# Packed attention with a top-1 mixture of experts: one count of tokens per expert behind the last batch, and the branch behind the loop with its sides exchanged

## The chip, the cores and the metric

The kernel runs on one core of a Trainium2 chip. The metric is the device time of one execution in microseconds (us); lower is better. Engines are named as the profile names them: PE is TensorE (PEld its weight loads), DVE is VectorE, ACT is ScalarE, POOL is GpSimd, SP is SyncE, which here only issues DMAs and waits. A name with a q (SPq, ACTq) is the engine's sequencer: waits, branches, register loads and DMA issues, which don't count as busy.

## The reference, cut to what matters

```python
def sm_attn(qq, kk, vv):
    s = scale * np.matmul(qq, kk.transpose(0, 1, 3, 2))
    a = np.exp(s - np.max(s, axis=-1, keepdims=True))
    a = a / (np.sum(a, axis=-1, keepdims=True) + 1e-09)
    return np.matmul(a, vv)
p_packed = sm_attn(p, k, v)          # batch 8, heads 8, 32 packed rows, head size 64
x = sm_attn(q, p_packed, p_packed)   # 576 tokens a batch, then (4608, 512)

expert_idx = np.argmax(xn @ en.T / tau, axis=1)   # 8 experts; xn, en: rows divided by their norms
for e in range(E):
    mask = expert_idx == e
    h = np.maximum(x[mask] @ w1[e], 0.0)
    out[mask] = gate_w[mask, None] * (h @ w2[e])
```

With these inputs the expert that the kernel guesses for a batch is that of all its 576 tokens: in the trace nothing of the path for missed tokens runs.

## The kernel before

The kernel takes the 8 batches one after the other. For each it **guesses** the expert of the whole batch from the packed rows (`guess`), runs that expert's feed-forward for all 576 tokens on PE (`ffn`), and lays the next batch's attention between the matmuls (`att1`, `att2`). `att2` ends with `route`, which computes for every token the logits of 8 experts and the sum of squares, and from them a one-hot matrix `oh` of the token's true expert. `gates` makes the gate weights of it.

Whether the guess held is checked. Per batch, `counts` multiplies a column of ones with `oh` in two small matmuls (L732: 32 columns, L735: 8 columns), so that PE adds up the tokens per expert into a PSUM tile of the ring `pf` (4 buffers), and DVE adds the five pieces (L737). `gates_main` then multiplies with the one-hot row `sel` of the guess (L1231) and sums (L1232) into `rest_f[b]`. Behind the loop DVE turns these into tokens that the guess missed (L1372 to L1378), and all five engines load the total into a register (L1379) and branch on it (L1380): over 0, a second, slow path runs batch by batch; at 0, which is the case here, the program ends. The slow path ("rest path" below) is a few hundred instructions an engine that stand in the program though none of them runs.

The order of the work is set by Python generators that are stepped by hand. `ffn` yields after every few matmuls and the loop at L1324 to L1369 steps the next batch's attention there; for batch 0 a table `PLAN` says which generator is stepped. All instructions are put out in that order and each engine runs its own in order. The names that the change and the prediction touch:

- `route` (L657 to L725): ten times a batch DVE reduces logits out of a PSUM tile `pt` (L695), and ACT squares the other columns of the same tile with a sum (L699; the trace shows it as an ACTIVATE and an ACTIVATION_READ_ACCUMULATOR). The squares themselves go to a tile `scr` that nothing reads; it has 2 buffers. ACT's square waits for DVE's reduce of the same piece, and DVE's next reduce out of the same PSUM bank waits for ACT's square.
- `w1_rows` (L831 to L857): PE multiplies packed rows with the first weights (L841), ACT takes the high part `G` (L854) and DVE the rest (L855), in turn, four times.
- `key_scores` (matmuls on L259 with `kt`): the first scores of a batch's attention; its second half writes the PSUM tile that the last L855 reads.
- `keys` (L284 to L286 on DVE): transposes of a batch's keys, which free the buffers `nat` into which SP loads (L174, L200). SP issues all its DMAs in order.
- At the end each engine that takes the branch at L1380 clears its semaphores (SP nine of them, each waiting for that queue's last DMA) and goes to the end block (L1479), where SP waits once more for everything and a barrier of all engines closes the program.

Of the kernel before, what the change touches and what calls it, by code (L numbers as in the profile page):

```python
# [17 lines left out]
P = 128  # L18
HB = 4
NC5 = 5  # L20
# [3 lines left out]
def kernel(  # L24
# [55 lines left out]
    for e in range(E):  # L80
        nc.vector.memset(ecol[:, e : e + 1], float(e))
    rest_f = cp.tile([1, B], F32, name="rest_f")
    rest_i = cp.tile([1, B + 1], I32, name="rest_i")

    def rsqrt(x, y, tag, eng=nc.vector):
# [66 lines left out]
    class Batch:  # L152
        def __init__(self):
            for name in ("kT", "qT", "s1", "mx", "p1", "sums", "rinv", "pp2", "s2", "p1T"):
                setattr(self, name, {})
            self.begun = self.soft = False

    def load_nat(b, n):

# [362 lines left out]
    def guess(x, late=0, engine=mybir.EngineType.Pool, total=None):  # L522
        pt = ps.tile([P, 512], F32, name="pu", tag="pf")
        if total is not None:

            for n in range(NPR):
                nc.tensor.matmul(
                    pt[:1, :E], total[:, n : n + 1], enT[:, n], start=(n == 0), stop=(n == NPR - 1)
                )
        else:  # L530
            for g in range(NG):
                nc.tensor.matmul(pt[:1, :E], itau, x.ppf[:, g, D:], start=(g == 0), stop=(g == NG - 1))
        yield
        m8 = sm.tile([1, 8], F32, name="m8", tag="m8")
        idx = sm.tile([1, 8], U32, name="idx", tag="idx")
        nc.vector.max(m8, pt[:1, :E])
        nc.vector.max_index(idx, m8, pt[:1, :E])
        gi = sm.tile([1, 1], F32, name="gi", tag="gi")
        nc.vector.tensor_copy(gi, idx[:, 0:1])
        x.sel = sm.tile([1, E], F32, name="sel", tag="sel")  # L540
        nc.vector.tensor_scalar(
            out=x.sel, in0=ecol[:1], scalar1=gi, scalar2=None, op0=ALU.is_equal
        )
        yield from idle(late)
        x.e = nc.values_load(idx[0:1, 0:1], engines=[engine], min_val=0, max_val=E - 1)
# [126 lines left out]
    def route(x, fine=False):  # L672
        lgs, sss = x.routed
        for c0, c1 in ((0, 2), (2, NC5)):
            pts = [pb.tile([P, 1024], F32, name="pt", tag="pb") for _ in range(2)]
            for c in range(c0, c1):
                for g in range(NG):
                    for n in range(2 * c, min(2 * c + 2, S // 64)):
                        for h in range(HB):
                            at = 512 * (h % 2) + 256 * g + XW * (c - c0)  # L680
                            nc.tensor.matmul(  # L681
                                pts[h // 2][64 * (n % 2) : 64 * (n % 2) + 64, at : at + XW],
                                x.at[32 * h : 32 * h + 32, g, 64 * n : 64 * n + 64],
                                x.ppf[32 * h : 32 * h + 32, g],
                                start=True,
                                stop=True,
                                tile_position=(32 * h, 64 * (n % 2)),
                            )
            yield
            views = [pt.rearrange("p (b s) -> p b s", s=256) for pt in pts]  # L690
            for c in range(c0, c1):
                r = rows(c)
                for m in range(2):
                    v = views[m][:r, :, XW * (c - c0) : XW * (c - c0) + XW]
                    nc.vector.tensor_reduce(  # L695
                        lgs[:r, m, c], v[:, :, D:].rearrange("p b e -> p e b"), axis=AX.X, op=ALU.add
                    )
                    scr = sb.tile([P, 4, D], F32, name="scr", tag="scr", bufs=2)
                    nc.scalar.activation(  # L699
                        scr[:r], v[:, :, :D], AF.Square, accum_out=sss[:r, m, c : c + 1]  # L700
                    )
                yield

        lg = sm.tile([P, NC5, E], F32, name="lgt", tag="lgt")
        ss = sm.tile([P, NC5], F32, name="sst", tag="sst")
        nc.vector.tensor_tensor(out=lg, in0=lgs[:, 0], in1=lgs[:, 1], op=ALU.add)
        nc.gpsimd.tensor_tensor(out=ss, in0=sss[:, 0], in1=sss[:, 1], op=ALU.add)
        x.lg, x.ss = lg, ss
        if fine:
            yield  # L710
        nc.vector.tensor_scalar_mul(lg, lg, itau)
        mx = sm.tile([P, NC5, 1], F32, name="lmx", tag="lmx")
        nc.vector.tensor_reduce(mx, lg, axis=AX.X, op=ALU.max)
        nc.vector.tensor_tensor(
            out=lg, in0=lg, in1=mx.broadcast_to([P, NC5, E]), op=ALU.subtract
        )
        oh = sm.tile([P, NC5, E], F32, name="oh", tag="oh")
        nc.vector.scalar_tensor_tensor(
            out=oh, in0=lg, scalar=0.0, in1=code.broadcast_to([P, NC5, E]),
            op0=ALU.is_ge, op1=ALU.mult,  # L720
        )
        nc.vector.tensor_reduce(mx, oh, axis=AX.X, op=ALU.max)
        nc.vector.tensor_tensor(
            out=oh, in0=code.broadcast_to([P, NC5, E]), in1=mx.broadcast_to([P, NC5, E]),
            op=ALU.is_equal,  # L725
        )
        x.oh = oh

    def counts(x):
        oh = x.oh  # L730
        pt = ps.tile([P, 512], F32, name="pu", tag="pf")
        nc.tensor.matmul(  # L732
            pt[:1, : 4 * E], ones, oh[:, 0:4].rearrange("p c e -> p (c e)"), start=True, stop=True
        )
        nc.tensor.matmul(pt[:1, 4 * E : 5 * E], ones[:64], oh[:64, 4], start=True, stop=True)  # L735
        cnt = sm.tile([1, E], F32, name="cnt", tag="cnt")
        nc.vector.tensor_reduce(  # L737
            cnt, pt[:1, : 5 * E].rearrange("p (c e) -> p e c", c=NC5), axis=AX.X, op=ALU.add
        )
        x.cnt = cnt  # L740


    def gates(x, eng=nc.vector):
# [263 lines left out]


    bat = [Batch() for _ in range(B)]
    NAT = 2 * NPR + NG  # L1010
    seq = [(b, i) for b in range(1, B) for i in range(NAT)]
    seq[NPR : 2 * NPR + NG] = [(1, i) for i in (8, 9, 4, 5, 6, 7)]
# [20 lines left out]
    def att_main(b):  # L1033
        x = bat[b]
        if b == 1:
            prefetch(5)
            yield from keys(x, nat_main(1), pns[1])
        if b:
            if b > 1:
                counts(bat[b - 1])  # L1040
            yield from att1(x, nat_main(b), b == 1)
            if b == 1:
                expert = guess(x)
                next(expert)
                query_scores(x)
                yield
            if b > 1:
                expert = guess(x)
                next(expert)
        second = att2(x, keys_main(b + 1) if b else None, b == 0, b == 1)  # L1050
        if b == 1:
            drain(expert)
            load_w1(x, x.e, queue=nc.gpsimd)
            yield
            yield next(second)
            yield next(second)
            load_w2(x, x.e, nc.gpsimd)
            route_tiles(x)
            yield next(second)
            yield next(second)  # L1060
        elif b:
            yield next(second)
            yield next(second)
            drain(expert)
            load_w1(x, x.e, queue=nc.gpsimd)
            yield next(second)
            load_w2(x, x.e, nc.gpsimd)
            route_tiles(x)
        yield from second
        x.soft = True  # L1070
        if b == B - 1:
            yield from idle(2)
            counts(x)

    def begin():

# [150 lines left out]
    def gates_main(b):  # L1227
        x = bat[b]
        yield from gates(x, nc.vector if b else nc.gpsimd)
        hit = sm.tile([1, E], F32, name="hit", tag="hit")  # L1230
        nc.vector.tensor_tensor(out=hit, in0=x.cnt, in1=x.sel, op=ALU.mult)  # L1231
        nc.vector.tensor_reduce(rest_f[:, b : b + 1], hit, axis=AX.X, op=ALU.add)  # L1232

    def store_main(b):
        x = bat[b]
# [70 lines left out]
    def route_first():  # L1306
        route_tiles(bat[0])
        yield from route(bat[0], True)
        yield
        counts(bat[0])  # L1310

    with tc.manual_schedule():
        begun = begin()
# [55 lines left out]
                    next(gate, None)  # L1369


    nc.vector.tensor_scalar(  # L1372
        out=rest_f, in0=rest_f, scalar1=-1.0, scalar2=float(S), op0=ALU.mult, op1=ALU.add
    )
    nc.vector.tensor_copy(rest_i[:, 0:B], rest_f)
    tot = sm.tile([1, 1], F32, name="tot")
    nc.vector.tensor_reduce(tot, rest_f, axis=AX.X, op=ALU.add)
    nc.vector.tensor_copy(rest_i[:, B : B + 1], tot)  # L1378
    n_rest = nc.values_load(rest_i[0:1, B : B + 1], min_val=0, max_val=B * S)  # L1379
    with tc.If(n_rest > 0):  # L1380
        with tc.For_i(0, B, 1) as b:
            nb = nc.values_load(rest_i[0:1, ds(b, 1)], min_val=0, max_val=S)
            with tc.If(nb > 0):
# [99 lines left out]
```

## Time and profile before

| | us |
|---|---|
| median of three runs | 439.41 (438.62 to 439.89) |
| the profiled execution, device time | 438.68 |
| its span, first to last instruction | 437.1 |
| outside the span | 1.6 |
| PE busy | 417.7 (96% of the span), 4802 instructions |
| PEld busy | 351.7 (80%) |
| DVE busy | 312.6 (72%) |
| ACT busy | 217.9 (50%) |
| POOL busy | 137.5 (31%) |
| DMA | 88.36 MB, mean 202 GB/s |

Busy times are shares of the whole span and overlap. The chain of work that ended last is followed back from the last instruction that did work; waits, branches and semaphores behind it stand in the span and not in the chain. A line number is that of the kernel before.

### The profile page before, as it was taken

The numbers are of one execution on the slowest core, as the hardware profiler recorded it, in microseconds if no ns is written. First come the engines' busy times: TensorE is split into PE (matmuls) and PEld (weight loads), VectorE is DVE, ScalarE is ACT, GpSimd is POOL, SyncE is SP. The second block draws the span as 40 slices with busy tenths as digits, with TensorE's granted clock in tenths as the row PEclk, the third lists the DMA queues.
The fourth block names the chain that finished last, engine by engine and source line by source line (L and its number), as shares of the span: only waits on it lengthen the run. The fifth ranks groups of instructions, "written<-read, shape, count | busy, mean of one in ns | idle before, by whom it ended". The sixth has DMA issues, their size and how long they took to land.

```text
span 437.1 us, 12609 instructions
## 1 busy us (share of the span) xinstructions
PE 417.7 (96%) x4802; PEld 351.7 (80%) x4803; DVE 312.6 (72%) x982; ACT 217.9 (50%) x652; POOL 137.5 (31%) x185
## 2 busy tenths in 40 slices
PE   7889996998999999999999999999999999999994
PEld 5646885688896889869896899859896898869993
DVE  4468678667996689868897589867897589656420
ACT  2456733665535744367534754367344664456300
POOL 2438743053212514044122424044041524035000
PEclk9899999799999999999999999999999999999998
DMA  7999989687897669965897668965798603731032
GB/s 198 294 292 281 247 232 264 189 188 172 251 359 206 152 192 305 310 167 128 249 362 204 153 178 270 326 180 135 215 335 246 170 16 102 287 74 36 2 63 53
DMA packets 47908, 88.36 MB, mean 202 GB/s; under 512 B 10904, under 2 KB 29400, under 8 KB 47840
## 3 DMA queue, kind: packets, MB, share of 16 engines
q1 hardware_dynamic: 39456, 57.83, 49.3%
q0 software_dynamic: 8000, 29.43, 19.5%
q8 instruction: 40, 0.66, 0.6%
q10 hardware_dynamic: 384, 0.21, 0.2%
q14 instruction: 28, 0.23, 0.2%
HBM read 78.00 MB, written 9.44 MB: 200 GB/s over the span
## 4 chain that ended last, share of the span: by engine, by line
PE 81%; DMA 7%; DVE 5%; ACT 3%; issue 1%; POOL 1%; SPq 1%; DVEq 0%; POOLq 0%; ACTq 0%
PE pf L951 24%; PE pf L969 19%; PE pf L923 19%; PE pt L259 4%; PE pt L681 4%; DMA nat<-in_v 3%; PE pt L841 3%; DMA nat<-in_q 2%; PE pt L384 2%; DMA nat<-in_k 2%; PE pt L364 1%; ACT scr L699 1%; PE pf L902 1%; PE pf L1179 1%; SPq L1251 1%
## 5 line engine op out<-in xcount | busy, mean ns | idle before, releaser
L817 POOL TENSOR_TENSOR w2s<-w2r,w2s 128x512 fp32r<-128x512 f32 x64 | 82.2, 1287 | 134.3 <-ACT w2s L816 133.0
L951 PE MATMUL pf<-hT,w2s 128*128 128x320 f32 x768 | 120.6, 312 | 0.0
L951 PEld LDWEIGHTS pf<-hT,w2s 128*128 128x128 f32 x768 | 113.0, 188 | 4.3 <-issue 3.3
L923 PE MATMUL pf<-AT,G 128*128 128x288 f32 x720 | 103.9, 298 | 0.1
L923 PEld LDWEIGHTS pf<-AT,G 128*128 128x128 f32 x720 | 97.3, 188 | 4.8 <-issue 2.3
L969 PE MATMUL pf<-w2s,hT 128*128 128x512 f32 (+1 forms) x408 | 96.7, 390 | 0.0
L969 PEld LDWEIGHTS pf<-w2s,hT 128*128 128x128 f32 x408 | 73.0, 191 | 20.8 <-issue 5.9
L926 DVE SCALAR_TENSOR_TENSOR hT<-pf,hT 128x288 fp32r<-128x288 f32 x128 | 56.3, 445 | 25.1 <-ACT hT L925 25.1
L925 ACT ACTIVATE hT<-pf 128x288 fp32r<-128x288 f32 x128 | 51.3, 415 | 39.2 <-PE pf L923 38.3
L699 ACT ACTIVATE scr<-pt 128x256 f32<-128x256 f32 (+1 forms) x80 | 29.8, 379 | 39.8 <-DVE lg L695 39.8
L816 ACT CAST w2s<-w2r 128x512 fp32r<-128x512 f32 x64 | 39.2, 624 | 6.3 <-issue 6.3
L792 POOL DMA_DIRECT2D w1t<-in_moe_w x14 | 10.7, 767 | 79.7 <-DVE st L588 75.1
L855 DVE TENSOR_TENSOR G<-pt,G 128x512 fp32r<-128x512 f32 x28 | 19.3, 690 | 17.4 <-ACT G L854 17.4
L778 ACT COPY gt<-gate 32x2 f32<-32x2 f32 (+1 forms) x128 | 24.6, 192 | 6.3 <-DVE gate L763 4.2
L1258 DVE STREAM_TRANSPOSE ot<-pf 128x320 f32<-128x320 f32 x32 | 16.0, 501 | 13.7 <-PE pf L951 11.5
L854 ACT CAST G<-pt 128x512 fp32r<-128x512 f32 x28 | 16.5, 589 | 17.6 <-DVE G L855 13.2
L609 ACT CAST AT<-at 128x576 fp32r<-128x576 f32 x16 | 10.8, 673 | 26.5 <-DVE at L606 25.4
L591 ACT ACTIVATE st<-st 128x576 f32<-128x576 f32 (+1 forms) x17 | 11.2, 658 | 24.0 <-issue 19.4
L681 PEld LDWEIGHTS pt<-ppf,at 32*64 32x64 f32 x1152 | 15.7, 136 | 8.9 <-ACT scr L699 4.4
L695 DVE TENSOR_REDUCE lg<-pt 128x8 f32<-128x32 f32 (+1 forms) x80 | 11.4, 175 | 15.8 <-PE pt L681 11.1
L681 PE MATMUL pt<-ppf,at 32*64 32x72 f32 x1152 | 18.4, 241 | 4.3 <-ACT scr L699 4.0
L289 DVE STREAM_TRANSPOSE kt<-nat 128x576 f32<-128x576 f32 x28 | 21.2, 762 | 0.0
(179 smaller groups left out, 491.9 us busy)
## 6 DMA issues: line engine op xcount, KB each, us to landing
nat<-in_k SPq DMA_DIRECT2D x112, 140.0 KB, 3.4
nat<-in_q SPq DMA_DIRECT2D x112, 140.0 KB, 5.0
w1t<-in_moe_w POOLq DMA_DIRECT2D x14, 1024.0 KB, 8.9
w2r<-in_moe_w POOLq DMA_DIRECT2D x28, 512.0 KB, 12.6
nat<-in_v SPq DMA_DIRECT2D x32, 160.0 KB, 3.8
out<-ot SPq DMA_DIRECT2D x28, 160.0 KB, 3.5
nat<-in_v SPq DMA_DIRECT2D x32, 128.0 KB, 3.7
out<-o SPq DMA_DIRECT2D x62, 64.0 KB, 1.7
```

The source lines that it names most:

```text
L289: nc.vector.transpose(kt.rearrange("p (n i) -> p n i", i=32), t)
L681: nc.tensor.matmul(pts[h // 2][64 * (n % 2) : 64 * (n % 2) + 64, at : at + XW], x.at[32 * h : 32 * h + 32, g, 64 * n : 64 * n + 64], x.ppf ...
L699: nc.scalar.activation(scr[:r], v[:, :, :D], AF.Square, accum_out=sss[:r, m, c : c + 1])
L778: copy(dst[32 * a : 32 * a + 32, k : k + HB * (n - 1) + 1 : HB], src[32 * k : 32 * k + 32, NCT : NCT + n],)
L816: nc.scalar.copy(hi, raw)
L817: eng.tensor_tensor(out=lo, in0=raw, in1=hi.bitcast(F32), op=ALU.subtract)
L855: nc.vector.tensor_tensor(out=x.G[:, 1, g, fs], in0=src, in1=x.G[:, 0, g, fs].bitcast(F32), op=ALU.subtract,)
L923: nc.tensor.matmul(pf[:, :HS], w, r, start=(n == 0), stop=(n == len(ops) - 1))
L925: nc.scalar.activation(hT[:, 0, f, cs], pf[:, :HS], AF.Relu)
L926: nc.vector.scalar_tensor_tensor(out=hT[:, 1, f, cs], in0=pf[:, :HS], scalar=0.0, in1=hT[:, 0, f, cs].bitcast(F32), op0=ALU.max, op1=ALU.s ...
L951: nc.tensor.matmul(pf[:, : S - TL], x.w2s[f][:, m, mt * P : mt * P + P], hT[:, a, f, TL:], start=(n == 0), stop=(n == len(ops) - 1),)
L969: nc.tensor.matmul(pf[:, :w], hT[:, a, f, c * P : (c + 1) * P], x.w2s[f][:, m, at : at + w], start=(f == 0 and i == 0), stop=(f == NF - 1 ...
```

## The change

- All batches' one-hot matrices go into one tile `hot` (128 x 8 x 5 x 8), all guessed rows into one tile `guessed`; both stay to the end.
- `counts` is no longer called in the main loop: eight calls (16 matmuls), eight reduces on DVE and eight pairs of `hit` instructions go. In their place `count_all` runs once, at the place of the last batch's `counts`: one matmul over 256 columns, one over 64, and nine DVE instructions, between which the generator yields. It also computes `rest_i`, so that the instructions behind the loop go.
- The tile `scr` has one buffer instead of two; the tile `cnts` of `count_all` shares it.
- The branch behind the loop gets `preferred_fallthrough_block=False`: the side for "nothing missed" stands right behind the branch, and the rest path behind that.

```diff
+    hot = cp.tile([P, B, NC5, E], F32, name="hot")
+    guessed = cp.tile([1, B, E], F32, name="guessed")
...
-                    scr = sb.tile([P, 4, D], F32, name="scr", tag="scr", bufs=2)
+                    scr = sb.tile([P, 4, D], F32, name="scr", tag="scr")
...
-        oh = sm.tile([P, NC5, E], F32, name="oh", tag="oh")
+        oh = x.oh if x.oh is not None else sm.tile([P, NC5, E], F32, name="oh", tag="oh")
...
+    def count_all():
+        pt = ps.tile([P, 512], F32, name="pu", tag="pf")
+        nc.tensor.matmul(
+            pt[:1, : B * 4 * E], ones, hot[:, :, 0:4].rearrange("p b c e -> p b (c e)"),
+            start=True, stop=True,
+        )
+        at = B * 4 * E
+        nc.tensor.matmul(
+            pt[:1, at : at + B * E], ones[:64], hot[:64, :, 4], start=True, stop=True
+        )
+        yield
+        cnt = sb.tile([1, B, E], F32, name="cnts", tag="scr")
+        nc.vector.tensor_reduce(
+            cnt, pt[:1, :at].rearrange("p (b c e) -> p b e c", b=B, c=4), axis=AX.X, op=ALU.add
+        )
+        yield
+        nc.vector.tensor_tensor(
+            out=cnt, in0=cnt, in1=pt[:1, at : at + B * E].rearrange("p (b e) -> p b e", b=B),
+            op=ALU.add,
+        )
+        yield
+        nc.vector.tensor_tensor(out=cnt, in0=cnt, in1=guessed, op=ALU.mult)
+        yield
+        nc.vector.tensor_reduce(rest_f.unsqueeze(2), cnt, axis=AX.X, op=ALU.add)
...
+    for b, x in enumerate(bat):
+        x.oh, x.sel = hot[:, b], guessed[:, b]
...
-            if b > 1:
-                counts(bat[b - 1])
             yield from att1(x, nat_main(b), b == 1)
...
         if b == B - 1:
             yield from idle(2)
-            counts(x)
+            yield from count_all()
...
         yield from gates(x, nc.vector if b else nc.gpsimd)
-        hit = sm.tile([1, E], F32, name="hit", tag="hit")
-        nc.vector.tensor_tensor(out=hit, in0=x.cnt, in1=x.sel, op=ALU.mult)
-        nc.vector.tensor_reduce(rest_f[:, b : b + 1], hit, axis=AX.X, op=ALU.add)
...
         yield from route(bat[0], True)
-        yield
-        counts(bat[0])
...
     n_rest = nc.values_load(rest_i[0:1, B : B + 1], min_val=0, max_val=B * S)
-    with tc.If(n_rest > 0):
+    with tc.If(n_rest > 0, preferred_fallthrough_block=False):
```

How the instructions stand, at three places. The names at a wait are semaphores: `Activation_49` is ACT's own count of finished instructions, `DVE_49` and `PE_49` those of the other engines.

**PE, between two batches in the middle of the run** (batches 2 and 3): the first weights of the next batch (L841), the rest of the second matmul, the next batch's first hidden block (L923), the counts, and the key scores (L259). Before:

```order
L969 MATMUL pf<-w2s,hT 128x512 x21
L841 MATMUL pt<-w1t,T 32x512 x16
L969 MATMUL pf<-w2s,hT 128x512 x15
L923 MATMUL pf<-AT,G 128x288 x6
L732 MATMUL pu<-oh,ones 1x32
L735 MATMUL pu<-oh,ones 1x8
L259 MATMUL pt<-kt,pw 32x288 x16
```

Changed (line numbers have moved; L1006, L878, L960 and L262 are the lines above):

```order
L1006 MATMUL pf<-w2s,hT 128x512 x21
L878 MATMUL pt<-w1t,T 32x512 x16
L1006 MATMUL pf<-w2s,hT 128x512 x15
L960 MATMUL pf<-AT,G 128x288 x6
L262 MATMUL pt<-kt,pw 32x288 x16
```

The two count matmuls are gone, and the key scores follow the hidden block at once.

**ACT, in the route of batch 0**, from the turned packed rows of batch 1 (`T`) on. Before:

```order
L485 COPY T<-pu 128x256 [waits PE_49]
L699 ACTIVATE scr,ss<-pt 128x256 [waits DVE_49] x4
L433 COPY ppf<-pu 128x2x8 [waits PE_49]
L699 ACTIVATE scr,ss<-pt 128x256 [waits DVE_49,PE_49,Activation_49] x2
L591 ACTIVATE st<-st 128x576 [waits DVE_49]
L699 ACTIVATE scr,ss<-pt 128x256 [waits DVE_49] x2
L699 ACTIVATE scr,ss<-pt 64x256 [waits DVE_49] x2
```

Changed (L701 is the square, L436 the copy of the logits, L593 the exponential):

```order
L488 COPY T<-pu 128x256 [waits PE_49]
L701 ACTIVATE scr,ss<-pt 128x256 [waits DVE_49]
L701 ACTIVATE scr,ss<-pt 128x256 [waits DVE_49,Activation_49] x3
L436 COPY ppf<-pu 128x2x8 [waits PE_49]
L701 ACTIVATE scr,ss<-pt 128x256 [waits DVE_49,PE_49,Activation_49] x2
L593 ACTIVATE st<-st 128x576 [waits DVE_49]
L701 ACTIVATE scr,ss<-pt 128x256 [waits DVE_49,Activation_49] x2
L701 ACTIVATE scr,ss<-pt 64x256 [waits DVE_49,Activation_49] x2
```

The order is the same, but nearly every square now waits for ACT's own count: for the square just before it, which wrote the only buffer.

**SP, at the end.** Before (the row that belongs to the other side, `L1380 UNCONDITIONAL_BRANCH`, is the last row of SP's program, with the end block behind it):

```order
L1379 TENSOR_LOAD rest_i
L1379 ISA x2
L1281 DMA out<-ot 32x10x128 x4
L1251 DMA out<-o 32x512 x6
L1380 COMPARE_AND_BRANCH
L1381 COMPARE_AND_BRANCH
```

Changed:

```order
L1404 TENSOR_LOAD rest_i
L1404 ISA x2
L1315 DMA out<-ot 32x10x128 x4
L1285 DMA out<-o 32x512 x6
L1405 COMPARE_AND_BRANCH
L1405 UNCONDITIONAL_BRANCH
L1406 COMPARE_AND_BRANCH
```

Waits are not rows of their own here: the nine semaphores of the side for "nothing missed" stand right before its unconditional branch. In both programs the end block stands last, behind the rest path, which on SP is 278 instructions long (252 on DVE, 499 on PE, 147 before and 154 changed on ACT, 96 on POOL). Before, the compare-and-branch jumps over it and the semaphores and the end block lie next to each other; in the changed program the semaphores follow the compare-and-branch, and the unconditional branch behind them jumps over the rest path.

## Rows read from the trace of the kernel before

**Rows 1.** The page: TensorE's granted clock in 40 slices of 10.9 us; the chain that ended last.
```profile
PEclk9899999799999999999999999999999999999998
...
PE 81%; DMA 7%; DVE 5%; ACT 3%; issue 1%; POOL 1%; SPq 1%; DVEq 0%; POOLq 0%; ACTq 0%
```
**Rows 2.** Instructions of the branch, L1380: duration ns min/median/max, first and last start us.
```profile
L1380 SPq EVENT_SEMAPHORE  x9: 17/17/17, 434.8 to 435.4; - x9
...
L1380 DVEq EVENT_SEMAPHORE  x2: 21/21/21, 423.6 to 423.7; - x2
...
L1380 ACTq EVENT_SEMAPHORE  x2: 17/17/17, 433.2 to 433.3; - x2
...
L1380 DVEq COMPARE_BRANCH  x1: 72/72/72, 420.7 to 420.7; - x1
L1380 PEldq COMPARE_BRANCH  x1: 3351/3351/3351, 429.0 to 429.0; - x1
L1380 SPq COMPARE_BRANCH  x1: 53/53/53, 432.0 to 432.0; - x1
L1380 ACTq COMPARE_BRANCH  x1: 54/54/54, 432.8 to 432.8; - x1
```
**Rows 3.** The last four stores, L1251 from 430 us on.
```profile
L1251 ACTq DMA_DIRECT2D out<-o x2: 383/406/428, 431.2 to 431.6; - x2
...
DMA to landing us min/median/max: 1.6/1.9/2.0
```
**Rows 4.** Timeline of PE, then PEld, from 143.3 us: start, us, engine and line [idle before].
```profile
144.12 0.22 PE L732 MATMUL pu<-oh,ones 128*1 128x32 f32 x2
...
144.28 0.15 PEld L259 LDWEIGHTS pt<-kt,pw 64*32 64x32 f32 x8
144.66 0.67 PEld L259 LDWEIGHTS pt<-kt,pw 64*32 64x32 f32 x24 [0.23 <-PE pu L735]
```
**Rows 5.** Timeline of DVE from 142.3 us, the last piece of G.
```profile
143.85 0.69 DVE L855 TENSOR_TENSOR G<-pt,G 128x512 fp32r<-128x512 f32 x1 [0.65 <-ACT G L854]
```
**Rows 6.** Timeline of PE at the last batch's count, and of float32 matmuls over 288 columns.
```profile
384.36 0.22 PE L732 MATMUL pu<-oh,ones 128*1 128x32 f32 x2
...
384.63 0.96 PE L969 MATMUL pf<-w2s,hT 128*128 128x512 f32 x3
...
26.99 2.18 PE L902 MATMUL pf<-at,g 128*128 128x288 f32 x8 [1.29 <-DVE at L606]
```
**Rows 7.** Timeline of ACT from 53.5 us: the first squares of batch 0.
```profile
54.51 0.38 ACT L699 ACTIVATE scr<-pt 128x256 f32<-128x256 f32 x1
54.79 0.19 ACT L699 ACTIVATION_READ_ACCUMULATOR scr<-pt 128x1 f32 x1
54.89 0.38 ACT L699 ACTIVATE scr<-pt 128x256 f32<-128x256 f32 x1
```
**Rows 8.** Timeline of PE, then DVE: who waits for the squares.
```profile
55.47 0.24 PE L532 MATMUL pu<-ppf,itau 128*1 128x8 f32 x4 [0.29 <-ACT ppf L433]
...
64.83 0.18 DVE L695 TENSOR_REDUCE lg<-pt 64x8 f32<-64x32 f32 x1 [0.18 <-ACT scr L699]
...
76.63 2.11 PE L681 MATMUL pt<-ppf,at 32*64 32x72 f32 x80 [4.01 <-ACT scr L699]
...
82.09 0.18 DVE L695 TENSOR_REDUCE lg<-pt 64x8 f32<-64x32 f32 x1 [0.18 <-ACT scr L699]
82.31 0.20 DVE L706 TENSOR_TENSOR lgt<-lg 128x40 f32<-128x40 f32 x1
```
**Rows 9.** SP's waits from 60 to 110 us; then timelines of SP, DVE and PE.
```profile
SPq L174 <- DVE kt L286: 13.3, 1, 13.3
...
85.31 0.78 SPq L174 DMA_DIRECT2D nat<-in_q  x2
...
89.40 0.65 DVE L855 TENSOR_TENSOR G<-pt,G 128x512 fp32r<-128x512 f32 x1
...
107.10 0.90 PE L384 MATMUL pt<-nat,p1T 128*32 128x64 f32 x40 [1.18 <-DMA nat<-in_v]
```

More of the change, by code (lines that the diff above doesn't have):

```diff
@@ L156, in __init__ @@
             self.begun = self.soft = False
+            self.oh = self.sel = None
     def load_nat(b, n):
@@ L539, in guess @@
         nc.vector.tensor_copy(gi, idx[:, 0:1])
-        x.sel = sm.tile([1, E], F32, name="sel", tag="sel")
         nc.vector.tensor_scalar(
@@ L740, in counts @@
         x.cnt = cnt
+    def count_all():
[22 more added lines that the diff above has]
+        nc.vector.tensor_reduce(rest_f.unsqueeze(2), cnt, axis=AX.X, op=ALU.add)
+        yield
+        nc.vector.tensor_scalar(
+            out=rest_f, in0=rest_f, scalar1=-1.0, scalar2=float(S), op0=ALU.mult, op1=ALU.add
+        )
+        yield
+        nc.vector.tensor_copy(rest_i[:, 0:B], rest_f)
+        tot = sm.tile([1, 1], F32, name="tot")
+        nc.vector.tensor_reduce(tot, rest_f, axis=AX.X, op=ALU.add)
+        yield
+        nc.vector.tensor_copy(rest_i[:, B : B + 1], tot)
     def gates(x, eng=nc.vector):
@@ L1369 @@
                     next(gate, None)
[L1372 to L1378, printed above, removed]
     n_rest = nc.values_load(rest_i[0:1, B : B + 1], min_val=0, max_val=B * S)
-    with tc.If(n_rest > 0):
+    with tc.If(n_rest > 0, preferred_fallthrough_block=False):
         with tc.For_i(0, B, 1) as b:
```

## The prediction

> **What bounds the kernel.** I read the chain first: PE holds 81% of it [rows 1], so an instruction that leaves another engine counts only where PE, or the end of the program, waits for it. Then I looked at the end, since the change touches the branch there; then at PE around the counts; then at who waits for the squares into `scr`, because the order shows new waits there.
>
> At the end the reader is to see that the span does not close with the last store. SP takes its branch at 432.0 and touches its first semaphore behind it at 434.8, although the branch itself takes 0.05 [rows 2]. DVE shows the same between 420.7 and 423.6, and PE's branch lasts 3.35. ACT takes 0.4 from 432.8 to 433.2 [rows 2]. The three with the long pause jump over 252 to 499 instructions of the rest path, ACT over 147: a far jump costs 2.7 to 3.35 us here, a near one 0.4. On SP this jump runs beside the last stores, which are issued until 431.6 and land within 2.0, so by 433.6 [rows 3]. When SP arrives at 434.8 its nine semaphores are all there, and it passes them by 435.4 [rows 2].
>
> **The end: +1.0 us.** In the changed program SP does not jump at the compare-and-branch. It reaches the nine semaphores at about 432.1 and stands there until the last store lands at 433.6; with one more semaphore it is through at 433.7. Only then comes the unconditional branch over the same 278 instructions. With SP's own price of 2.7 the end block starts at 436.4 instead of 435.4: +1.0. What was hidden beside the stores now stands behind them. Bounds: with PE's 3.35 it is +1.7; with a jump that costs only its own 0.05 it is 433.8 against 435.4, a gain of 1.6. I take SP's own row, since it is the same engine and distance. The other engines jump too, but have time: PE's last work is over 4 us ahead of the end block, and the barrier waits for SP. [...] The rows have 2.7 for a conditional branch at this distance and none for an unconditional one; I keep the row.
>
> **The counts on PE: 0 in the middle.** The two count matmuls hold PE's weight loads from 144.12 to 144.28, so 0.16 a batch [rows 4]. But the second half of the key scores starts only at 144.66 [rows 4]: it writes the PSUM tile that DVE's last L855 reads, and that ends at 143.85 + 0.69 = 144.54 [rows 5]. That chain of ACT and DVE hangs on L841, which PE ran before the counts and which stays as far ahead. So PE arrives 0.16 earlier and waits 0.16 longer. This wait stands in five of the six batches; in the first one the piece of G ends just as PE comes. Batch 0's own count, too, goes ahead of a wait of 1.18 for a load at 107.10 [rows 9], which takes its gain. Bounds: 0 and 7 x 0.16 = 1.1 us of gain. I take 0. The DVE instructions that go (three a batch) were not what PE waited for.
>
> **The one count: +0.5.** At the last batch the count stays where it was, and nothing holds PE back there: the next matmul follows at 384.63 [rows 6]. Its columns grow from 40 to 320, so by 280, close to the 288 of L902. There 8 records, two for a matmul, take 2.18 us [rows 6]: 0.27 a record, 0.54 a matmul, and 0.53 for 280 columns. I take +0.5 (0.4 to 0.6, as the last record's pipeline end is in it). The nine DVE instructions behind it lie in pauses of about 0.65 in which DVE waits for ACT's halves of G [rows 5], as the yields place them.
>
> **One buffer for `scr`: +1.4.** Now a square starts while the one before is still being read out: from 54.51 to 54.89 are 0.38 [rows 7]. In the changed order nearly every square waits for the one before, to the end of its read-out: 54.79 + 0.19 - 54.51 = 0.47. No row has ACT waiting for its own last result; on DVE the hand-over from a result (82.09 + 0.18) to its reader (82.31) is 0.04 [rows 8]. So a square takes 0.51 instead of 0.38: +0.13, bounded by 0.09 (no hand-over) and 0.2. Eighty squares would be 10 us, but in the middle batches they come in pairs with room behind them and PE doesn't wait for them. In the first two routes it does, and those places lie in line:
> - At 55.47 PE waits for ACT's L433 [rows 8], which follows four squares in ACT's queue. Three new waits: +0.4, for PE and for DVE's unpacking behind it.
> - At 64.83 DVE's reduce waits for a square [rows 8]. Two new waits lie before it: +0.3. From there DVE has no pause to take it up before the next burst at 75.
> - At 76.63 PE has waited 4.01 for a square [rows 8], the third of a burst of four. The fourth, the pair behind it and the next lead to DVE's last reduce at 82.09, which again waits for a square [rows 8]. Five new waits in line: +0.7. That DVE no longer stops at 80.7 for the first count doesn't help: ACT's queue comes later than that.
>
> So DVE's tail of the route (L706) moves from 82.31 by 0.4 + 0.3 + 0.7 = 1.4, and with it the keys' transposes. Two things hang on these. SP waits 13.3 for one of them and issues from 85.31 on [rows 9]; its queue then runs to the values of batch 2, for which PE waits 1.18 at 107.10 [rows 9]. And DVE's first L855, at 89.40 [rows 9], stands behind the last transpose, and the chain of rows 5 behind that. Either way PE is 1.4 late at 107. A PE that is late before 107 would have cost nothing by itself, since the load takes it up; the load being late is what costs. Later batches have no such wait for a load. Bounds: 0 if SP's queue or the load has slack that I don't see, 2.1 with 0.2 a square.
>
> **The sum.** 1.0 + 0 + 0.5 + 1.4 = +2.9. The profiled execution took 438.7, so 441.6. The median of the three runs, 439.4, stands 0.7 above it; a median is what is forecast: 442.3. Own range 441.4 to 443.6.
>
> **The rivals.**
> - *The jump is free* (not slower). SP stands 1.5 us in its semaphores and the branch behind them has no condition; if its target is fetched in that time, the end gains 1.6. For it: ACT's 0.4 shows that a target at hand is cheap [rows 2]. Against: nothing fetched ahead for three engines whose targets lay as far. 1.4 + 0.5 - 1.6 = +0.3: 439.7. It decides as soon as the jump costs under about 1 us. [...]
> - *The squares stay hidden.* If the later transposes don't make the load at 107 late, PE's delay before it is taken up by that wait. 1.0 + 0.5 = +1.5: 440.9. For it: PE waits there anyway. Against: SP's 13.3 names the transposes.
> - *Both, and PE gets its slots back.* If in addition the G chain moves up with PE, -1.6 + 0.5 - 1.1 = -2.2: 437.2.
> [...]
>
> **Numbers.** Forecast 0.52, hidden squares 0.17, free jump 0.15, both with the slots 0.11, the clock 0.05. A difference under 0.3% (1.3 us) can't be told from none here. Faster: 0.11. Same: the free jump and a third of the hidden squares, 0.21. Slower: 0.52 + 0.11 + 0.05 = 0.68. The range from 439.4 to 443.6 takes in the free jump, the hidden squares and the forecast's own range, and leaves out the other two.
>
> **What would show it.** Right: SP's nine semaphores begin right behind its compare-and-branch, not 2.7 later, and a pause over 2.5 follows the unconditional branch behind them; squares 0.51 apart; the wait for values at 107 ends 1.4 later; the key scores' second half still starts with the end of L855; 0.5 more at the last count. Wrong: no pause behind SP's unconditional branch, or the load at 107 where it was.

## The result, and the profile of the changed kernel

| | before | changed |
|---|---|---|
| median of ten runs, us | 438.75 (436.99 to 439.89) | 442.25 (440.73 to 444.17) |
| ratio of the times, 95% interval | | 1.0078 (1.0058 to 1.0099) |
| profiled execution, its span | 438.68, 437.1 | 442.42, 440.8 |
| SP's first branch behind the loop | 432.0 | 432.7 |
| from there to the end of the span | 5.1 | 8.1 |

The change makes the kernel 0.8% slower: 3.5 us at the medians, where +2.9 was forecast. The last two rows say where: of the 3.7 us between the two profiled executions 0.65 had come together when SP reached its branch, and 3.1 came behind it.

The end, instructions of the branch (L1405, before L1380) and of the end block (L1504, before L1479), with the columns of [rows 2], and the last four stores as in [rows 3]. An engine now has two rows of the branch, the compare-and-branch and the unconditional branch behind its semaphores:

```profile
L1405 SPq EVENT_SEMAPHORE  x9: 17/17/17, 432.8 to 436.0; - x9
...
L1405 PEldq COMPARE_BRANCH  x2: 95/1987/3879, 429.6 to 431.7; - x2
L1405 PEldq EVENT_SEMAPHORE  x2: 51/51/51, 431.3 to 431.5; - x2
L1405 SPq COMPARE_BRANCH  x2: 38/48/57, 432.7 to 436.1; - x2
L1405 ACTq COMPARE_BRANCH  x2: 38/46/53, 433.4 to 433.7; - x2
...
L1504 SPq EVENT_SEMAPHORE  x14: 17/28/28, 439.2 to 440.7; - x14
...
L1504 ACTq DRAIN  x2: 8/44/81, 436.2 to 440.2; - x2
...
L1285 ACTq DMA_DIRECT2D out<-o x2: 383/406/428, 431.8 to 432.3; - x2
...
DMA to landing us min/median/max: 3.3/3.5/3.5
```

The nine semaphores now begin at once (432.8), as forecast. But they end at 436.0, not 1.7 behind the branch: the stores land 3.3 to 3.5 after their issue instead of 1.6 to 2.0 [rows 3]. Then comes the second branch at 436.1, and the end block begins at 439.2, 3.1 later. PE's row shows what else moved: its long jump (3.88) begins at 431.7, behind its own two semaphores, where before it began at 429.0 [rows 2]. The DMA view of 432.5 to 434.5 us, the time in which most packets of the stores run, lists what moved then (queue, kind: packets, MB, share of the 16 engines):

```profile
q10 hardware_dynamic: 91, 0.13, 26.6%
q1 hardware_dynamic: 93, 0.13, 22.1%
q8 instruction: 1, 0.02, 4.3%
```

Beside the stores (q1 and q10) there is a piece of code on q8, 16 KB that take 1.4 us (4.3% of 16 engines in 2.0 us). Before, in 431.9 to 433.15 us, when the stores ran, q8 had none: its piece had come between 429.9 and 430.9, ahead of the stores' issue at 431.2. The same view of 433.9 to 435.0 us, after q8's piece has ended, shows what is left of the stores:

```profile
q1 hardware_dynamic: 6, 0.01, 3.5%
...
q10 hardware_dynamic: 6, 0.01, 2.7%
```

These twelve packets move one after the other, the first at 433.9 and the last at 434.9; all others were done by 433.9. It looks as if they had stood behind the piece of code on one of the 16 engines, but the records don't name the engine of a packet.

PE and its weight loads at the places of the forecast:

```profile
55.95 0.24 PE L535 MATMUL pu<-ppf,itau 128*1 128x8 f32 x4 [0.70 <-ACT ppf L436]
...
77.39 2.25 PE L683 MATMUL pt<-ppf,at 32*64 32x72 f32 x80 [4.34 <-ACT scr L701]
...
107.89 0.84 PE L387 MATMUL pt<-nat,p1T 128*32 128x64 f32 x36 [0.87 <-DMA nat<-in_v]
...
144.90 0.15 PEld L262 LDWEIGHTS pt<-kt,pw 64*32 64x32 f32 x8 [0.16 <-PE pf L960]
145.44 0.67 PEld L262 LDWEIGHTS pt<-kt,pw 64*32 64x32 f32 x24 [0.39 <-issue]
...
384.55 0.59 PE L746 MATMUL pu<-hot,ones 128*1 128x256 f32 x2
385.07 0.27 PE L751 MATMUL pu<-hot,ones 64*1 64x64 f32 x2
385.27 0.97 PE L1006 MATMUL pf<-w2s,hT 128*128 128x512 f32 x3
```

Before, these stood at 55.47, 76.63, 107.10, 144.28, 144.66, 384.36 (the first count matmul) and 384.63 (the matmul behind the count) [rows 4, 6, 8, 9]; the row of 385.07 is the second count matmul. ACT's squares, DVE and SP:

```profile
54.35 0.38 ACT L701 ACTIVATE scr<-pt 128x256 f32<-128x256 f32 x1
54.63 0.19 ACT L701 ACTIVATION_READ_ACCUMULATOR scr<-pt 128x1 f32 x1
54.86 0.38 ACT L701 ACTIVATE scr<-pt 128x256 f32<-128x256 f32 x1
...
83.49 0.20 DVE L708 TENSOR_TENSOR lgt<-lg 128x40 f32<-128x40 f32 x1
...
144.63 0.69 DVE L892 TENSOR_TENSOR G<-pt,G 128x512 fp32r<-128x512 f32 x1 [0.65 <-ACT G L891]
...
SPq L177 <- DVE kt L289: 11.2, 1, 11.2
...
86.50 0.78 SPq L177 DMA_DIRECT2D nat<-in_q  x2
```

The squares stand 0.51 apart, the tail of the route and SP's queue 1.2 later than before [rows 8, 9].

One wait of before is gone. In batch 6 the key scores' second half had begun 1.35 behind the first, where in batches 3, 4, 5 and 7 it begins 0.41 behind it. DVE, POOL and PE of before around it (the DVE instructions are of the route of batch 5, which ends shortly before):

```profile
286.57 1.29 DVE L718 SCALAR_TENSOR_TENSOR oh<-lgt,code 128x40 f32<-128x40 f32 x1
...
288.13 1.13 DVE L723 TENSOR_TENSOR oh<-code,lmx 128x40 f32<-128x40 f32 x1
...
286.54 1.27 POOL L817 TENSOR_TENSOR w2s<-w2r,w2s 128x512 fp32r<-128x512 f32 x1 [15.73 <-ACT w2s L816]
...
287.93 1.28 POOL L817 TENSOR_TENSOR w2s<-w2r,w2s 128x512 fp32r<-128x512 f32 x1
...
294.28 1.17 PE L259 MATMUL pt<-kt,pw 64*32 64x288 f32 x24 [0.67 <-DVE cnt L737]
```

and the same DVE instructions, POOL's first and PE's key scores in the changed kernel:

```profile
287.37 0.20 DVE L720 SCALAR_TENSOR_TENSOR hot<-lgt,code 128x40 f32<-128x40 f32 x1
...
287.83 0.20 DVE L725 TENSOR_TENSOR hot<-code,lmx 128x40 f32<-128x40 f32 x1
...
287.90 1.27 POOL L854 TENSOR_TENSOR w2s<-w2r,w2s 128x512 fp32r<-128x512 f32 x1 [16.32 <-ACT w2s L853]
...
293.92 1.75 PE L262 MATMUL pt<-kt,pw 64*32 64x288 f32 x32
```

Before, two DVE instructions that can take 0.20 took 1.29 and 1.13; each ended 0.05 behind a POOL instruction that it met. L718 began 0.03 after POOL's; in the other seven batches it takes 0.20 (in batches 2, 3, 4 and 6 L723 is held too, but not L718). In the changed kernel the first is over before POOL begins, and the second, which began 0.07 before POOL, takes its 0.20. The profile puts PE's wait down to L737, the reduce of the count. But PE begins 0.15 behind the end of the last piece of G with that reduce and without it: 293.45 + 0.69 to 294.28 before (L855), 293.65 + 0.69 to 294.49 in the changed kernel (L892). So it waited for G, whose chain on DVE stands behind the two slow instructions.

### The profile page after: what moved, and what is told of

Same layout as the page of the kernel before. It is cut to its first block, busy times and chain, and to the rows that moved or that the text cites. A ratio compares the mean times of both kernels' runs of the same rounds, so it can differ in the third digit from the quotient of the medians.

```text
span 440.8 us, 12594 instructions
## 1 busy us (share of the span) xinstructions
PE 420.0 (95%) x4774; PEld 351.4 (80%) x4775; DVE 305.2 (69%) x962; ACT 223.5 (51%) x652; POOL 138.4 (31%) x185
## 4 chain that ended last, share of the span: by engine, by line
PE 80%; DMA 6%; SPq 4%; ACT 3%; DVE 2%; issue 2%; POOL 1%; DVEq 0%; ACTq 0%; POOLq 0%
PE pf L988 24%; PE pf L960 19%; PE pf L1006 18%; PE pt L262 4%; PE pt L683 3%; DMA nat<-in_v 3%; PE pt L878 3%; PE pt L387 2%; ACT scr L701 2%; DMA nat<-in_k 2%; DMA nat<-in_q 1%; PE pt L367 1%; SPq L177 1%; PE pf L939 1%; SPq L1285 1%
## 5 line engine op out<-in xcount | busy, mean ns | idle before, releaser
L960 PE MATMUL pf<-AT,G 128*128 128x288 f32 x720 | 103.8, 298 | 0.1
L960 PEld LDWEIGHTS pf<-AT,G 128*128 128x128 f32 x720 | 97.3, 188 | 4.8 <-issue 2.8
L1006 PE MATMUL pf<-w2s,hT 128*128 128x512 f32 (+1 forms) x408 | 96.8, 391 | 0.0
L1006 PEld LDWEIGHTS pf<-w2s,hT 128*128 128x128 f32 x408 | 73.5, 192 | 21.2 <-issue 5.9
L701 ACT ACTIVATE scr<-pt 128x256 f32<-128x256 f32 (+1 forms) x80 | 30.6, 383 | 40.0 <-DVE lg L697 37.9
L892 DVE TENSOR_TENSOR G<-pt,G 128x512 fp32r<-128x512 f32 x28 | 19.3, 690 | 20.9 <-ACT G L891 20.9
L593 ACT ACTIVATE st<-st 128x576 f32<-128x576 f32 (+1 forms) x17 | 11.2, 657 | 20.8 <-issue 17.4
```

The lines of the kernel that those rows point to most:

```text
L701: nc.scalar.activation(scr[:r], v[:, :, :D], AF.Square, accum_out=sss[:r, m, c : c + 1])
L892: nc.vector.tensor_tensor(out=x.G[:, 1, g, fs], in0=src, in1=x.G[:, 0, g, fs].bitcast(F32), op=ALU.subtract,)
L960: nc.tensor.matmul(pf[:, :HS], w, r, start=(n == 0), stop=(n == len(ops) - 1))
L1006: nc.tensor.matmul(pf[:, :w], hT[:, a, f, c * P : (c + 1) * P], x.w2s[f][:, m, at : at + w], start=(f == 0 and i == 0), stop=(f == NF - 1 ...
```

## The experiments

Two questions were open: what makes the stores land late and the end 3.1 longer, and where the forecast's +1.9 of the body went, of which SP's branch shows 0.65. A second theory stood against the forecast's: PE's far jump now waits for PE's last matmul (its semaphores stand ahead of it), so PE's code is fetched just when the last stores run, and they wait behind it. Each timed ratio below is against runs of the kernel before on the same chip.

### The end

**The layout alone** (kernel before):

```diff
-    with tc.If(n_rest > 0):
+    with tc.If(n_rest > 0, preferred_fallthrough_block=False):
```

> The kernel before with one edit: the branch behind the loop laid out the other way. Forecast's theory (SP's jump of 2.7 us comes behind the stores, which land within 2.0 of their issue as before): +1.0 us, from SP's first branch to the end of the span 6.1 instead of 5.1. Second theory, formed on the trace of the change (PE's jump now comes behind PE's last matmul, so the fetch of its code falls among the last stores and holds them): the four stores land 3.3 to 3.5 after their issue, 8.1 from SP's branch to the end, +3.0 in the time. Third (the late stores of that one execution were chance): +1.4, stores at 1.6 to 2.0.

Measured: 441.28 against 438.98, ratio 1.0053 (1.0035 to 1.0072). The branch, the end block and the stores of this kernel:

```profile
L1380 SPq EVENT_SEMAPHORE  x9: 17/17/17, 432.0 to 435.3; - x9
...
L1380 PEldq COMPARE_BRANCH  x2: 95/2102/4108, 428.9 to 430.9; - x2
...
L1380 SPq COMPARE_BRANCH  x2: 38/48/57, 431.9 to 435.4; - x2
...
L1479 SPq EVENT_SEMAPHORE  x14: 17/28/28, 437.9 to 439.5; - x14
...
DMA to landing us min/median/max: 3.4/3.5/3.6
```

The late stores come with the layout, in a second kernel. The end is 7.6 long: +2.5 on the span and +2.3 in the time (the second theory had 8.1 and +3.0), so most of what the whole change costs. Here too twelve packets of the stores are left when q8's piece ends at 433.4, and they move one after the other until 434.5. ACT's jump takes only 0.5 (432.9 to 433.4), and DVE's lies at 421.7 to 425.2, long before the stores, so that PE's is the one long jump among them.

**PE's distance and SP's, apart.** Three kernels with the new layout. The first cuts the rest path of the kernel with the layout alone down to its loop, a zero tile and the stores; the second moves the rest path's DMAs from SP to POOL and leaves PE's 499 instructions; the third is the first with SP's distance given back. Of each edit some lines are shown:

```diff
-                drain(keys(x, nat, pn))
...
-                        drain(ffn(x, (store, turn_tail, lambda: iter(()))))
                 for c in range(NCT):
...
```

> The kernel before with the new layout (as the run with the layout alone) and with the rest path cut to its loop, a zero tile and the stores: attention, routing and feed-forward of missed tokens are left out of it (nothing of it runs here). All engines then jump over 32 to 99 instructions. If the jump's price is the distance (second theory): 0.4 behind SP's last branch instead of 2.5 to 3.1, no code of PE fetched among the stores, stores landing within 2.0; from SP's first branch to the end 4.2 instead of 7.6, about 0.9 faster than before. If a jump costs 2.5 at any distance: stores at 2.0, 6.2 to the end, +1.1. If the layout itself makes the stores late: 5.5, +0.4.

```diff
...
-                        nc.sync.dma_start(
+                        nc.gpsimd.dma_start(
                             out_tokens(b)[:, HB * c + a],
...
```

> The same edit in the new layout: SP near, PE still far. Second theory, with two causes apart: PE's code is still fetched among the stores, which land 3.3 to 3.5 after issue, but SP's last jump costs 0.4: from SP's first branch to the end 5.1 to 5.5 instead of 7.6, 0 to +0.4 against before. If the late stores were SP's own doing: they land within 2.0, 4.2 to the end, 0.9 faster. If the jump's price isn't its distance: 7.6 to the end, +2.4.

```diff
...
+                for _ in range(9):
+                    for c in range(NCT):
+                        for a in range(HB):
...
```

> The run with the short rest path and the new layout, with the rest path's stores written nine times instead of once: SP jumps over 291 instructions again, PE, DVE, ACT and POOL over 32 to 37. Second theory: the stores land within 2.0 of their issue, as no code of PE is fetched among them, SP is through its semaphores 1.8 behind its first branch, and its last jump costs 2.5 to 3.1: 6.0 to 6.7 from SP's first branch to the end, against 3.95 with SP near and 7.6 with both far; +1.0 to +1.6 against before. If SP's far jump itself made the stores late: 7.6, +2.5. If PE's distance decided the price of SP's jump: 4.0, 1.4 faster.

| new layout | SP jumps over | PE jumps over | stores land in | SP's branch to end | ratio (95%) |
|---|---|---|---|---|---|
| layout alone | 278 | 499 | 3.4 to 3.6 | 7.6 | 1.0053 (1.0035 to 1.0072) |
| SP near | 154 | 499 | 2.9 to 3.0 | 6.5 | 1.0036 (1.0019 to 1.0053) |
| PE near | 291 | 32 | 1.6 to 1.9 | 6.1 | 1.0023 (1.0012 to 1.0033) |
| both near | 99 | 32 | 1.6 to 1.9 | 3.9 | 0.9961 (0.9945 to 0.9978) |

Both near, then PE near with SP far, then SP near with PE far (there L1385 is the branch and L1485 the end block):

```profile
L1380 SPq EVENT_SEMAPHORE  x9: 17/17/17, 431.1 to 432.7; - x9
...
L1380 PEldq COMPARE_BRANCH  x2: 90/141/192, 427.9 to 428.2; - x2
L1380 SPq COMPARE_BRANCH  x2: 38/48/57, 430.9 to 432.7; - x2
...
L1430 SPq EVENT_SEMAPHORE  x14: 17/28/28, 433.3 to 434.8; - x14
```

```profile
L1380 SPq EVENT_SEMAPHORE  x9: 17/17/17, 431.8 to 433.4; - x9
...
L1380 SPq COMPARE_BRANCH  x2: 38/48/57, 431.7 to 433.4; - x2
...
L1431 SPq EVENT_SEMAPHORE  x14: 17/28/28, 436.1 to 437.7; - x14
```

```profile
L1385 SPq EVENT_SEMAPHORE  x7: 17/17/17, 432.6 to 435.1; - x7
...
L1385 PEldq COMPARE_BRANCH  x2: 95/1756/3418, 429.4 to 431.4; - x2
...
L1385 SPq COMPARE_BRANCH  x2: 38/48/57, 432.5 to 435.2; - x2
...
L1485 SPq EVENT_SEMAPHORE  x14: 17/28/28, 435.7 to 438.9; - x14
```

The price of SP's jump goes with SP's distance: 0.5 us from the second branch to the end block over 99 and over 154 instructions (432.74 to 433.25 and 435.2 to 435.7), 2.5 to 3.1 over 278 and 291. The number of instructions alone doesn't set the price, though. ACT's jump over 147 took 0.4 to 0.5 in the kernels with the whole rest path and two buffers; over the 154 of the three kernels with one buffer it took 2.5 (433.7 to 436.2 in the changed kernel) to 2.9, where SP over 154 took 0.5. ACT was still done before SP, so this cost nothing. The late stores go with PE's distance and not with SP's: with PE near they land in 1.6 to 1.9, however far SP jumps. In the DMA view of 431.5 to 434.0 us of the kernel with PE near and SP far, when its stores run, q8 is missing:

```profile
q10 hardware_dynamic: 96, 0.13, 22.2%
q1 hardware_dynamic: 96, 0.13, 17.8%
```

So both parts of the second theory are shown. With PE near and SP far the end is what the forecast had for the change: +1.0 on the span, and 1.0023 in the time. DVE and ACT became near together with PE; that it is PE's code follows from q8, from the time of PE's branch, and from the layout alone, where ACT's jump is short and DVE's long over. One expectation was missed: with SP near and PE far the end is 6.5, not 5.1 to 5.5, because the end block itself took 3.2 (435.7 to 438.9) instead of 1.6. The trace has the difference in one place. Nine of the fourteen semaphores are done at 436.3, and from 436.3 on there are

```profile
L1485 SPq EVENT_SEMAPHORE  x5: 17/28/28, 437.9 to 438.9; - x5
```

In this pause of 1.6 one piece of code, of 8 KB, comes on another queue (q14). That it is SP's next code is likely, but was not tested.

**SP near in the old layout.** The same move of the DMAs to POOL, in the kernel before:

> The kernel before, with the old layout, and the rest path's DMAs issued by POOL instead of SP: SP jumps over 154 instructions instead of 278, POOL over 243 instead of 96, PE over 499 as before. Price by distance: SP's first semaphore 0.4 to 0.5 behind its branch instead of 2.7, then it waits for the last store (1.6 behind the branch) and is through 2.2 behind it: 3.8 to the end instead of 5.1, 1.3 faster. POOL's jump lies at 409 and costs nothing. If 154 is still far: 2.7 as before, no change.

Measured: 437.24 against 438.74, ratio 0.9962 (0.9949 to 0.9975). Its semaphores begin 0.5 behind SP's branch and end 1.6 behind it:

```profile
L1385 SPq EVENT_SEMAPHORE  x7: 17/17/17, 433.0 to 434.1; - x7
...
L1385 SPq COMPARE_BRANCH  x1: 53/53/53, 432.5 to 432.5; - x1
```

The jump in the old layout was not wholly hidden by the stores: 1.5 us of it could be had in the time (1.1 from SP's branch to the end in the trace).

### The body

**One buffer for `scr` alone** (kernel before):

```diff
-                    scr = sb.tile([P, 4, D], F32, name="scr", tag="scr", bufs=2)
+                    scr = sb.tile([P, 4, D], F32, name="scr", tag="scr")
```

> The kernel before with one edit: one buffer for scr. Squares 0.51 apart instead of 0.37. Forecast's theory: PE late by 1.4 behind the load near 107 us and for good, +1.4. Second theory (what the trace of the change has): late by 0.8 behind that load, and the 0.7 wait in the key scores of batch 6, where two DVE instructions of the route took 1.1 to 1.3 us beside a POOL instruction, goes or stays by how the two happen to meet: +0.2 to +0.8. Third (squares hidden): 0. The tail stays as before, 5.1 from SP's branch to the end.

**The one count alone** (the change with the old layout, and):

```diff
-                    scr = sb.tile([P, 4, D], F32, name="scr", tag="scr")
+                    scr = sb.tile([P, 4, D], mybir.dt.bfloat16, name="scr", tag="scr", bufs=2)
...
```

> The change without its layout and with two buffers for scr (of 16-bit floats, so that they fit; nothing reads them): the one count alone. Forecast's theory: +0.5 at the last batch's count and nothing elsewhere, since PE waits for G in each batch: +0.5. Rival (the slots come back to PE): 0.5 - 1.1 = -0.6. With the wait in batch 6 gone, as in the trace of the change: 0.5 - 0.6 = -0.1.

**The change with the old layout, and the change with two buffers**:

> The change with the branch laid out as before. Both theories leave the tail at 5.1 from SP's branch to the end, with the stores landing 1.6 to 2.0 after issue. Forecast's theory: 1.4 + 0.5 = +1.9 against before. Second theory: 0.8 + 0.4 - 0.6 = +0.6, as PE stood in the trace of the change at SP's branch, and so 3.0 faster than the change.

> The change with two buffers for scr (of 16-bit floats): its squares alone are undone. Forecast's theory: 1.4 faster than the change, 440.8. By the two runs with the old layout (439.4 with one buffer, 438.4 with two): 1.0 faster, 441.2. If the squares are hidden: 442.2, as the change. Behind the load at 107 us PE should stand where it stood before, and SP's end stay at 7.6 to 8.1 behind its first branch.

| | time, before beside it | ratio (95%) |
|---|---|---|
| one buffer alone | 439.36, 438.98 | 1.0009 (0.9996 to 1.0022) |
| one count alone | 438.41, 438.98 | 0.9989 (0.9974 to 1.0003) |
| change, old layout | 439.44, 438.98 | 1.0010 (0.9998 to 1.0022) |
| change, two buffers | 441.50, 438.37 | 1.0060 (1.0042 to 1.0077) |

Without its layout the change costs 0.5, within the noise of one comparison. One buffer costs 1.0 where the two kernels with the old layout are set against each other (439.44 and 438.41), 0.4 beside the counts of before (within the noise), and 0.4 in the change itself (+3.5 with it, +3.1 with two buffers; 441.5 lies between the expected 441.2 and the 442.2 of hidden squares). The 16-bit type by itself changes nothing on ACT: a square takes 0.38 with either.

The one count alone is 0.6 faster, which is also what the rival of PE's slots coming back would give. The traces decide against it: from batch 3 to 4 and from 4 to 5 the key scores stand 49.54 and 49.55 apart before, and 49.55 and 49.55 with the one count.

The times alone don't say why the body costs so little. The traces do, in three stretches of PE, over all twelve kernels. From the first route matmul of batch 0 (50.93 before) to the key scores' second half in batch 3 (144.69): 92.8 to 94.1 us in the six kernels with the old counts and two buffers, 93.0 to 93.4 in the three with the one count and two buffers, 95.1 with one buffer alone, 94.5 and 94.6 in the two with both. So, by the means, one buffer costs 1.2 to 1.6 there beside the same counts, and the one count nothing; one execution of each kernel stands behind this, and the six spread over 1.3. From there to the same place in batch 6: 149.6 in those six kernels, 148.7 to 149.0 in all others. And from there to SP's branch: 137.7 with the old counts, 138.2 with the one count, in every kernel.

So the middle stretch gives back 0.6 to 0.9 to any kernel that has either edit, and that is batch 6: in all six traces of the first kind both DVE instructions of the route met POOL's and took about 1.3 and 1.1, in the other six at most one of them did, and PE's long wait in the key scores is in the first six and in none of the others. What makes either edit shift DVE by the few tenths that decide was not tried.

### The version that keeps what gained

The one count with two 16-bit buffers, the old layout, and the rest path's DMAs on POOL:

> A version that keeps what gained: the one count, two buffers for scr of 16-bit floats, the old layout, and the rest path's DMAs on POOL. By the run with the one count (0.6 faster) and the expectation of SP's near jump (1.3 faster): 1.9 faster than before, about 437.1; 0.6 faster if 154 instructions are still far.

Measured: 436.89 against 438.74, ratio 0.9954 (0.9936 to 0.9972): faster than both kernels, 1.9 us before the kernel before. From SP's branch to the end are 3.7.

## Why the prediction was right, and where it was not

The time was forecast well (442.3 against 442.25, and +2.9 against +3.5), but with luck: two steps had errors that partly cancel, 2.1 too little at the end and 1.25 too much in the body, and the median of three runs on which the sum was put stands 0.7 above that of ten (438.75).

- **The end: +3.1 instead of +1.0.** SP's semaphores and its jump behind them came as forecast, and the jump cost 3.1 (2.5 with the layout alone) where SP's own 2.7 was taken. What failed is the sentence "The other engines jump too, but have time". It asked when PE would arrive at the end block, not what PE's jump does on the way: its 16 KB of code come on a DMA queue at the time of the last stores. That held the stores by 1.6, so the term is about 1.0 + 1.6 + 0.4, the last from the jump. With PE near it is +1.0 as forecast. The end had been the largest gain among the rivals (a free jump); a near jump is nearly free, 0.5, but this one is far.
- **The unconditional branch.** The trace of the changed kernel has 38 ns for the instruction itself on SP (at 436.1), but the next one comes 3.1 us later. In the kernels with the new layout it is 0.5 to 3.1, by where the next one lies.
- **The squares: the mechanism right, the size nearly so.** 0.51 apart as forecast; PE at 55.95 (+0.48, forecast +0.4); the tail of the route at 83.49 (+1.2, forecast +1.4); SP at 86.50 (+1.2). PE's wait for the values at 107 ended 0.8 later in this execution, where 1.4 was forecast, and the stretch to batch 3 is 1.0 longer than the mean (93.45) of the six kernels without the edits. The rival that the squares stay hidden falls; why of SP's 1.2 only 0.8 reached PE was not looked into.
- **The counts in the middle: 0 held, but for batch 6.** At batch 3 the first half starts 0.62 later than before and the second half 0.78: PE arrived 0.16 earlier and waited 0.16 longer, up to the end of L892 (144.63 + 0.69 = 145.32). What failed is that the step took one batch for all: "So PE arrives 0.16 earlier and waits 0.16 longer" misses batch 6, where before had a wait that was 0.9 longer than in the batches beside it, and which either edit takes away. That gave 0.6 back in this execution and 0.9 in the other kernels. The row of that wait stood in the trace of before; its cause, two DVE instructions six times too long, was a coincidence that a small shift of DVE undoes.
- **The two slow instructions.** In the rows of batch 6 L718 began 0.03 behind POOL's instruction and ended 0.05 behind its end, and L725 of the changed kernel, 0.07 ahead of POOL's, was not held and took its 0.20.
- **The one count: +0.45** (the next matmul at 385.27 instead of 384.63, of which 0.19 was there at its start), forecast +0.5.
- **The clock.** No run shows the term that stands in the chances with 0.05. The kernel before has one slice of TensorE's granted clock at 0.7 [rows 1]. The changed kernel has one at 0.6, from 77.1 us, and no other below 0.9 up to the last, in which PE's work ends (0.7, before 0.8). From 88 to 430 us it is 1.00 in both, and the mean of the execution is 0.986 against 0.985.

The sum by what was measured in the one execution: 0.8 - 0.6 + 0.45 = +0.65 at SP's branch, and +3.1 behind it, 3.7.

## What to carry to other kernels

Look at where the target of a branch at the end of a program lies, and at what the jump runs beside. Here SP's jump over 278 instructions, moved behind the wait for the stores, cost 2.5 to 3.1 us there, and the 16 KB of code that came for PE's jump beside the last stores made them land in 3.3 to 3.5 us instead of 1.6 to 2.0. Where a path that rarely runs is long, shorten it on the engine that closes the program (its DMAs can be issued by an engine that is done early: 0.9962 here) rather than exchange the sides (1.0053). And before a small delay is summed up to the end, look for the waits downstream that will take it up, those by coincidence too.

## What was not expected

- Code for a far jump of PE, fetched beside four stores of 64 KB, made them land in 3.3 to 3.5 us instead of 1.6 to 2.0.
- A jump of SP over 154 instructions cost 0.5, over 278 2.5 to 3.1; ACT's cost 0.4 to 0.5 over 147 and 2.5 to 2.9 over 154. So the price doesn't rise at one number of instructions for all engines, and what sets it stays open.
- With SP near and PE far, SP needed 3.2 instead of 1.6 for the same fourteen semaphores of the end block, with one pause of 1.6 and a piece of code that came in it. Why stays open.
